# Float64 feed-forward weights written out as two ready parts, loaded straight into the last stage, and that stage's first product issued before the experts' last accumulation

## The chip, the cores and the metric

The kernel runs on one core of a Trainium2 chip. The metric is the device time of the whole program in microseconds, the median of three runs. TensorE (PE) multiplies, VectorE (DVE), ScalarE (ACT) and GpSimd (POOL) do elementwise work, and all DMA transfers are issued by SyncE (SP), whose queue takes them in order.

## The reference

Attention with a decay feeds eight experts whose outputs are summed with a gate that a few rounds of normalising produce, and their sum feeds one dense layer with a mish activation. Only the last two parts matter here.

```python
def _moe_ref(x, w_gate, w1, w2):          # x [1152, 512], w1 [8, 512, 1024], w2 [8, 1024, 512]
    ...
    for e in range(E):
        h = np.maximum(x @ w1[e], 0.0)
        ye = h @ w2[e]
        out += P[:, e:e + 1] * ye
    return out.astype(np.float32)

def _moe2_ref(x, w_in, w_out):            # w_in [512, 2048], w_out [2048, 512], both float64
    h = x @ w_in
    sp = np.where(h > 20.0, h, np.log1p(np.exp(np.minimum(h, 20.0))))
    g = h * np.tanh(sp)
    return (g @ w_out).astype(np.float32)
```

`w_in` and `w_out` become float64 through the division by a numpy square root, so the kernel receives them as 64-bit words.

## The kernel before, in words

Every product is made of three: a float32 operand is split into a high part, rounded to the multiplier's format, and a low part, the difference, and the product is high by high, high by low and low by high (`l1`, `l2`).

**Weights.** They come in halves of 512 hidden columns: halves 0 to 15 are the experts' (two each), halves 16 to 19 the dense layer's. Four slots hold four halves, half n in slot n modulo 4, each with the tiles `w1h`, `w1l`, `w2h` and `w2l`, 1 MB each. A half comes in four loads of 512 KB into the staging tile `stg` (L76). `split` then makes each part in two pieces: ScalarE copies 512 columns into the high tile (L89), and VectorE, or GpSimd where `lo_engine` says so, subtracts (L90). Such pieces wait in the list `bg` and one is taken out in each step.

**Experts.** A step is one `l1` (12 matmuls of 384 columns into `ph`), its `relu_split` (ScalarE `hh`, VectorE `hlo`), then the `l2` of the step before (9 matmuls of 512 columns into three accumulators). There are 184 steps. After the last step of an expert and a chunk of 384 tokens, `evict` adds the three accumulators to `acc` on VectorE (L799). In the last expert, `x2_trans` transposes the finished chunks 0 and 1 on TensorE (L818), and ScalarE and VectorE write them to `xh` and `xl`, the inputs of the last stage.

**Decoding.** Between steps 11 and 137, at odd steps, `decode` turns one piece of a float64 matrix (128 x 256 words) into float32 with eight VectorE instructions and writes it to DRAM (`w_in_f`, `w_out_f`, 64 pieces of 128 KB). Halves 16 to 19 are then loaded from there and split like the others: 16 and 17 during the last expert, with VectorE subtracting, and 18 and 19 in the first eight steps of the last stage, with GpSimd subtracting, two pieces per step.

**Last stage.** There are 48 steps, three chunks of 16 groups; call them u0 to u47. Each has an `l1`, ten elementwise instructions of the mish (VectorE L885, L892, L901, L905, L906, L907, L914; ScalarE L886, L893, L894 and the copy `hh` at L909, which the VectorE subtraction `hlo` at L914 follows), and an `l2`. The code issues the `l1` of a step and then the `l2` of the step three earlier. Before the first `l1` stand four `x2_trans` of chunk 2, since its accumulators are only complete then. The scratch tiles of the mish are the accumulators `acc` 0 to 5 and two tiles `scr`.

Every engine takes its instructions in the order of the code; nothing reorders them.

Of the kernel before, what the change touches and what calls it, by code (L numbers as in the profile page):

```python
# [18 lines left out]
F2 = 2048  # L19
# [19 lines left out]
def f(ap):  # L39
    return ap.bitcast(F32)  # L40


class Weights:
    """Half-expert weights: DMA to staging, split into hi + lo, ring of slots."""

    def __init__(self, nc, stage, w1, w2, w_in, w_out):
        self.nc, self.stage = nc, stage
        self.src = (w1, w2, w_in, w_out)
        self.slots = {}
        self.raw = {}  # L50

# [6 lines left out]
        return self.slots[half % 4]  # L58

    def load(self, half, part):  # L60
        w1, w2, w_in, w_out = self.src
        t = self.stage.tile([128, 2, 512], F32, tag="stg", name="stg")
        kk = part % 2
        if half < 2 * E:
            e, a = divmod(half, 2)
            if part < 2:
                src = w1[e, kk * 256:(kk + 1) * 256, a * 512:(a + 1) * 512]
            else:
                src = w2[e, a * 512 + kk * 256:a * 512 + (kk + 1) * 256, :]
        else:  # L70
            a = half - 2 * E
            if part < 2:
                src = w_in[kk * 256:(kk + 1) * 256, a * 512:(a + 1) * 512]
            else:
                src = w_out[a * 512 + kk * 256:a * 512 + (kk + 1) * 256, :]
        self.nc.sync.dma_start(out=t, in_=src.rearrange("(k p) n -> p k n", p=128))  # L76
        self.raw[half, part] = t

    def split(self, half, part, j, lo_engine=None, how=None):
        nc = self.nc  # L80
# [18 lines left out]
def attention_moe_kernel(  # L99
# [23 lines left out]

    xh = [xpool.tile([128, KD, CH], FR, name=f"xh{c}") for c in range(NCH)]
    xl = [xpool.tile([128, KD, CH], FR, name=f"xl{c}") for c in range(NCH)]
    w_in_f = dram.tile([DM, F2], F32, name="w_in_f")
    w_out_f = dram.tile([F2, DM], F32, name="w_out_f")
    wts = Weights(nc, stage, w1, w2, w_in_f, w_out_f)
    wts.add_slot(0, slot_a)

    idn = const.tile([128, 128], F32, name="idn")
# [502 lines left out]
    for i in (1, 2, 3):  # L634
        wts.add_slot(i, slot_b)
    acc += [accb.tile([128, DM], F32, name=f"acc{j}") for j in range(6, NT)]
    ps_h = mctx.enter_context(tc.tile_pool(name="ps_h", bufs=2, space=PSUM))
    ps_a = mctx.enter_context(tc.tile_pool(name="ps_a", bufs=5, space=PSUM))
    ps_m = mctx.enter_context(tc.tile_pool(name="ps_m", bufs=1, space=PSUM))

    def l1(half, ft_, c):
        w = wts.get(half)
        fs = slice(ft_ * 128, (ft_ + 1) * 128)
        ph = ps_h.tile([128, 512], F32, tag="h", name="ph")[:, :CH]
        for kk in range(KD):
# [68 lines left out]
        raw64.append((raw, dst, j))  # L714

    def decode():
        """One piece of a float64 matrix, taken as its raw words, to float32 (nearest even)."""
        raw, dst, j = raw64.pop()
        d2 = dst.rearrange("(p a) n -> p (a n)", p=128)
        a_ = dec.tile([128, 256], F32, tag="da", name="da")  # L720
        b_ = dec.tile([128, 256], F32, tag="db", name="db")
        ai, bi = a_.bitcast(U32), b_.bitcast(U32)
        lw, hw = raw[:, :, 0], raw[:, :, 1]
        v = nc.vector
        v.tensor_scalar(out=ai, in0=hw, scalar1=0x7FFFFFFF, scalar2=None, op0=ALU.bitwise_and)
        v.tensor_scalar(out=a_, in0=a_, scalar1=TINY, scalar2=HUGE, op0=ALU.max, op1=ALU.min)
        v.tensor_scalar(
            out=ai, in0=ai, scalar1=0x38000000, scalar2=4, op0=ALU.bitwise_xor, op1=ALU.logical_shift_left
        )
        v.tensor_scalar(out=bi, in0=hw, scalar1=0x80000000, scalar2=None, op0=ALU.bitwise_and)  # L730
        v.scalar_tensor_tensor(
            out=ai, in0=ai, scalar=1, in1=bi, op0=ALU.logical_shift_right, op1=ALU.bitwise_or
        )
        v.tensor_scalar(out=bi, in0=ai, scalar1=0xFF800000, scalar2=None, op0=ALU.bitwise_and)
        v.scalar_tensor_tensor(out=b_, in0=lw, scalar=2.0 ** -52, in1=b_, op0=ALU.mult, op1=ALU.mult)
        v.tensor_tensor(out=a_, in0=a_, in1=b_, op=ALU.add)
        nc.sync.dma_start(out=d2[:, j * 256:(j + 1) * 256], in_=a_)
        if decodes:
            fetch(*decodes.pop(0))

    decodes = [(w_in, w_in_f, j) for j in range(DM * F2 // (128 * 256))]
    decodes += [(w_out, w_out_f, j) for j in range(DM * F2 // (128 * 256))]
    bg = []
    dmaq = []
    side = [sinkhorn()]
# [32 lines left out]
    for half in range(2, 20):  # L778
        queue_load(half)
    queue_split(1, nc.gpsimd)  # L780
    psa = {}
# [45 lines left out]
    for idx, (e, c, g, first, last) in enumerate(steps):  # L827
        if first and (c == 0 and e > 0 or idx == 0):
            if e < E - 1:
                queue_split(2 * e + 2)  # L830
                queue_split(2 * e + 3)
            else:
                queue_split(16)
                queue_split(17)
        if c > 0 and g == 2 and e == E - 1:
            tq += [(c - 1, kk) for kk in range(KD)]
        half, gg = 2 * e + g // 4, g % 4
        ph = l1(half, gg, c)
# [19 lines left out]
    l2(*prev[0])
    evict(*prev[1])
    mctx.close()  # L860

# [1 line left out]
    fctx = ExitStack()  # L863
    ps_h = fctx.enter_context(tc.tile_pool(name="ps_h2", bufs=4, space=PSUM))
    ps_a = fctx.enter_context(tc.tile_pool(name="ps_a2", bufs=4, space=PSUM))
    for t in bg:
        t()
    bg.clear()
    queue_split(18, nc.gpsimd)
    queue_split(19, nc.gpsimd)  # L870
    scr2 = fctx.enter_context(tc.tile_pool(name="scr2", bufs=1))
    free = [a_[:, :CH] for a_ in acc[:6]] + [scr2.tile([128, CH], F32, name=f"scr{i}") for i in range(2)]
    scr = {"m": free[:1], "e": free[1:4], "w": free[4:6], "a": free[6:8]}

    def scratch(tag):
        t = scr[tag].pop(0)
        scr[tag].append(t)
        return t

    osb = acc[6:9]  # L880

    def mish_a(u):
        m = scratch("m")
        e_ = scratch("e")
        nc.vector.tensor_scalar(out=m, in0=u["ph"], scalar1=20.0, scalar2=None, op0=ALU.min)  # L885
        nc.scalar.activation(out=e_, in_=m, func=AF.Exp)  # L886
        u["e"] = e_

    def mish_w(u):
        e_ = u["e"]  # L890
# [23 lines left out]
        nc.vector.tensor_tensor(out=hl, in0=u["g"], in1=f(u["hh"]), op=ALU.subtract)  # L914
        u["hl"] = hl

    for kk in range(KD):
        x2_trans(NCH - 1, kk, ps_h, "h")
    steps = [(c, g) for c in range(NCH) for g in range(F2 // 128)]

    def finish(c):
# [9 lines left out]
    for idx in range(len(steps) + 3):  # L931
# [8 lines left out]
        if idx < len(steps):  # L940
            c, g = steps[idx]
            half, gg = 16 + g // 4, g % 4
            u = dict(half=half, gg=gg, c=c, first=g == 0, last=g == F2 // 128 - 1)
            us.append(u)
            u["ph"] = l1(half, gg, c)
        if idx < len(steps):
            mish_a(u)
        if 2 <= idx < len(steps) or idx == len(steps) + 1:
            mish_d(us[idx - 2])
        if idx < len(steps):  # L950
            for _ in range(2):
                if bg:
                    bg.pop(0)()
# [39 lines left out]
```

## Time and profile before

| | |
|---|---|
| device time, median of 3 runs | 1175.01 us (1175.01 to 1175.04) |
| span of the profiled execution | 1173.7 us |
| TensorE busy | 1138.0 us (97%) |
| VectorE busy | 732.7 us (62%) |
| ScalarE busy | 392.3 us (33%) |
| GpSimd busy | 119.0 us (10%) |
| DMA | 82.08 MB, mean 70 GB/s |

The profile is of one execution and shows its span, from the first instruction to the last; it does not show a separate time of that execution, so the 1.3 us between span and median stand for what lies around it. Busy shares are means over stages with different limits: attention lasts to about 185 us, the experts to about 953 us, the last stage to the end. A busy TensorE is not TensorE at its peak, since matmuls overlap and their ends are modelled; the distance from the start of one group of matmuls to the start of the next says more.

### The profile page before, as it was taken

To read this page: it belongs to the slowest core of one execution; us is meant where nothing else is said; L and a number is where in the kernel's file an instruction comes from. 1 tells how busy PE (TensorE), PEld (TensorE's weight loads), DVE (VectorE), ACT (ScalarE), POOL (GpSimd) and SP (SyncE) were. 2 spreads that over 40 slices of the span, in tenths; PEclk is the share of its full clock that TensorE was granted. 3 is DMA by queue.
4 is the path that set the end of the run, shared out by engine and by line. 5 is a ranking of instruction groups with operands and counts; after the bars stand their busy time and mean duration, and the time that the engine had idled before them with its cause. 6 is when DMAs were issued, how large, how long until landed. Compare 5 with 4: busy or idle time off the path is not lost.

```text
span 1173.7 us, 16305 instructions
## 1 busy us (share of the span) xinstructions
PE 1138.0 (97%) x6200; PEld 1010.1 (86%) x6200; DVE 732.7 (62%) x1707; ACT 392.3 (33%) x832; POOL 119.0 (10%) x143
## 2 busy tenths in 40 slices
PE   5899999999999999999999999999999988999998
PEld 4677788999999999999999999999999976899997
DVE  7866655776646655664665575533134259998887
ACT  6756653322212211221221221122123235555554
POOL 5734433000000000000000000000000015100000
PEclk9989999999999999999999999999999999999999
DMA  6424212333313321331332232212011012000000
GB/s 153 113 48 94 52 47 66 104 114 109 114 53 100 102 90 61 125 95 55 112 108 64 86 118 85 63 56 71 1 54 61 30 35 74 1 28 1 27 1 27
DMA packets 77759, 82.08 MB, mean 70 GB/s; under 512 B 34912, under 2 KB 46944, under 8 KB 77680
## 3 DMA queue, kind: packets, MB, share of 16 engines
q1 hardware_dynamic: 77680, 81.03, 23.1%
q8 instruction: 49, 0.80, 0.3%
q14 instruction: 30, 0.25, 0.1%
HBM read 66.00 MB, written 10.82 MB: 65 GB/s over the span
## 4 chain that ended last, share of the span: by engine, by line
PE 91%; DVE 6%; ACT 1%; issue 1%; DMA 1%; POOL 0%; SPq 0%; ACTq 0%; DVEq 0%; POOLq 0%
PE ph L647 39%; PE pa L667 39%; PE x L430 3%; PE pt L406 2%; PE sp L354 2%; PE pa L499 2%; PE ph L480 2%; PE pt L318 1%; PE sp L355 1%; DVE scr L905 1%; DVE scr L906 1%; DVE scr L907 0%; DVE acc L892 0%; DVE scr L901 0%; ACT hh L909 0%
## 5 line engine op out<-in xcount | busy, mean ns | idle before, releaser
L647 PE MATMUL ph<-xh,w1h 128*128 128x384 f32 x928 | 312.3, 337 | 0.2 <-DVE xl L822 0.2
L647 PE MATMUL ph<-xh,w1l 128*128 128x384 f32 x928 | 311.8, 336 | 0.0
L647 PE MATMUL ph<-xl,w1h 128*128 128x384 f32 x928 | 311.3, 335 | 0.0
L657 DVE SCALAR_TENSOR_TENSOR hlo<-ph,hh 128x384 fp32r<-128x384 f32 x184 | 102.8, 558 | 317.6 <-ACT hh L656 317.6
L656 ACT ACTIVATE hh<-ph 128x384 fp32r<-128x384 f32 x184 | 90.7, 493 | 588.9 <-PE ph L647 581.7
L667 PE MATMUL pa<-w2h,hh 128*128 128x512 f32 x696 | 274.1, 394 | 10.6 <-ACT hh L909 10.6
L667 PE MATMUL pa<-w2l,hh 128*128 128x512 f32 x696 | 273.4, 393 | 0.0
L667 PE MATMUL pa<-w2h,hlo 128*128 128x512 f32 x696 | 272.9, 392 | 0.0
L647 PEld LDWEIGHTS ph<-xh,w1h 128*128 128x128 f32 x928 | 174.3, 188 | 9.4 <-DVE xl L822 0.5
L647 PEld LDWEIGHTS ph<-xl,w1h 128*128 128x128 f32 x928 | 174.3, 188 | 8.5
L647 PEld LDWEIGHTS ph<-xh,w1l 128*128 128x128 f32 x928 | 174.3, 188 | 0.0
L667 PEld LDWEIGHTS pa<-w2h,hh 128*128 128x128 f32 x696 | 131.0, 188 | 33.0 <-ACT hh L909 13.4
L667 PEld LDWEIGHTS pa<-w2h,hlo 128*128 128x128 f32 x696 | 131.0, 188 | 30.4 <-DVE hlo L914 2.6
L667 PEld LDWEIGHTS pa<-w2l,hh 128*128 128x128 f32 x696 | 131.2, 188 | 19.1
L90 POOL TENSOR_TENSOR w1l<-stg,w1h 128x512 fp32r<-128x512 f32 x12 | 17.4, 1473 | 782.1 <-DVE acc L892 756.7
L390 POOL TENSOR_SCALAR p<-p,rs 128x256 f32<-128x256 f32 (+6 forms) x80 | 46.6, 594 | 66.9 <-DVE rs L386 41.5
L377 ACT ACTIVATE p<-p,nmax 128x256 f32<-128x256 f32 (+6 forms) x80 | 48.2, 604 | 9.6 <-DVE nmax L367 8.7
L799 DVE SCALAR_TENSOR_TENSOR acc<-pa,P,acc 128x512 f32<-128x512 f32 x69 | 47.5, 743 | 1.7 <-PE pa L667 1.7
L367 DVE CUSTOM_DVE_ANT_0 p<-sp,mask 128x256 f32<-128x256 f32 (+6 forms) x80 | 38.0, 476 | 12.6 <-PE sp L355 10.5
L89 ACT CAST w1h<-stg 128x512 fp32r<-128x512 f32 x76 | 45.8, 612 | 0.0
L89 ACT CAST w2h<-stg 128x512 fp32r<-128x512 f32 x76 | 45.8, 612 | 0.0
L90 DVE TENSOR_TENSOR w1l<-stg,w1h 128x512 fp32r<-128x512 f32 x64 | 44.1, 692 | 0.1
(150 smaller groups left out, 1200.0 us busy)
## 6 DMA issues: line engine op xcount, KB each, us to landing
stg<-in_moe_w_dram SPq DMA_DIRECT2D x64, 512.0 KB
raw<-in_moe_w_in_dram SPq DMA_DIRECT2D x32, 256.0 KB
raw<-in_moe_w_out_dram SPq DMA_DIRECT2D x32, 256.0 KB
w_in_f<-da SPq DMA_DIRECT2D x32, 128.0 KB
w_out_f<-da SPq DMA_DIRECT2D x32, 128.0 KB
stg<-w_in_f SPq DMA_DIRECT2D x8, 512.0 KB
stg<-w_out_f SPq DMA_DIRECT2D x8, 512.0 KB
out_dram<-acc SPq DMA_DIRECT2D x9, 256.0 KB
```

Of the source, the lines that this page charges most:

```text
L89: nc.scalar.copy(out=hi, in_=raw)
L90: (lo_engine or nc.vector).tensor_tensor(out=lo, in0=raw, in1=f(hi), op=ALU.subtract)
L354: nc.tensor.matmul(out=t[:n, :w], lhsT=a1, rhs=kt[:, h, ks], start=True, stop=False)
L367: nc.vector.tensor_tensor_reduce(out=p[:n, a, o:o + w], in0=t[:n, :w], in1=mask[:n, m0 + o:m0 + o + w], scale=-1.0, scalar=prev, op0=ALU.a ...
L377: nc.scalar.activation(out=p[:n, a, :nk], in_=p[:n, a, :nk], func=AF.Exp, bias=prev, scale=-1.0, accum_out=u["ssum"][:n, a:a + 1],)
L390: nc.gpsimd.tensor_scalar(out=p[:n, a, :nk], in0=p[:n, a, :nk], scalar1=r[:n, a:a + 1], scalar2=1.0, op0=ALU.mult, op1=ALU.mult,)
L430: nc.tensor.matmul(out=x[64 * a:64 * a + 64, h // 2, :n], lhsT=vts[b, j][:w, h + a, :], rhs=pT[:w, a, j * n:(j + 1) * n], start=j == 0, st ...
L647: nc.tensor.matmul(out=ph, lhsT=w[wn][:, kk, fs], rhs=x[c][:, kk], start=(kk == 0 and n == 0), stop=(kk == KD - 1 and n == 2),)
L656: nc.scalar.activation(out=hh, in_=ph, func=AF.Relu)
L657: nc.vector.scalar_tensor_tensor(out=hl, in0=ph, scalar=0.0, in1=f(hh), op0=ALU.max, op1=ALU.subtract)
L667: nc.tensor.matmul(out=pa[j], lhsT=a_[:, ts_], rhs=w[wn][:, ft_, :], start=(first and n == 0), stop=(last and n == 2),)
L799: nc.vector.scalar_tensor_tensor(out=acc[t], in0=pa, scalar=sc, in1=acc[t], op0=ALU.mult, op1=ALU.add)
```

## The change

`decode` no longer writes its float32 piece. At the following even step a new function `part` makes the high part on ScalarE and the low part on VectorE, 256 columns each, and writes both to DRAM; there are now four DRAM tensors, `w_in_h`, `w_in_l`, `w_out_h` and `w_out_l`. A new method `direct` loads a half of the dense layer with four DMAs of 1 MB straight into its slot, with no staging and no `split`. Halves 16 and 17 are issued at step (7, 1, 0), 15 steps before the experts' last; half 18 after the experts' last step and half 19 after its accumulation.

The first `l1` of the last stage, u0, is issued before the experts' last `l2`, with the first two of its mish instructions, and its `ph` comes from the experts' pool. The four `x2_trans` of chunk 2 move from in front of the last stage into its steps 7, 9, 11 and 13; they are needed from step 32 on.

```diff
+    def direct(self, half):
+        a = half - 2 * E
+        for n, src in (("w1", self.ready[0]), ("w2", self.ready[1])):
+            for m, s in zip("hl", src):
+                s = s[:, a * 512:(a + 1) * 512] if n == "w1" else s[a * 512:(a + 1) * 512, :]
+                self.nc.sync.dma_start(
+                    out=f(self.get(half)[n + m]), in_=s.rearrange("(k p) n -> p k n", p=128)
+                )
...
-        nc.sync.dma_start(out=d2[:, j * 256:(j + 1) * 256], in_=a_)
         if decodes:
             fetch(*decodes.pop(0))
+        decoded.append((a_, b_, dst, j))
+
+    def part():
+        a_, b_, dst, j = decoded.pop()
+        nc.scalar.copy(out=b_.bitcast(FR), in_=a_)
+        nc.vector.tensor_tensor(out=a_.bitcast(FR), in0=a_, in1=b_, op=ALU.subtract)
+        for t, d in zip((b_, a_), dst):
+            d2 = d.rearrange("(p a) n -> p (a n)", p=128)
+            nc.sync.dma_start(out=d2[:, j * 256:(j + 1) * 256], in_=t)
...
-            else:
-                queue_split(16)
-                queue_split(17)
...
+        if e == E - 1 and c == 1 and g == 0:
+            wts.direct(16)
+            wts.direct(17)
...
             decode()
+        elif decoded:
+            part()
...
-    queue_split(18, nc.gpsimd)
-    queue_split(19, nc.gpsimd)
...
+    wts.direct(18)
+    u0 = dict(half=2 * E, gg=0, c=0, first=True, last=False, ph=l1(2 * E, 0, 0))
+    mish_a(u0)
     l2(*prev[0])
     evict(*prev[1])
+    wts.direct(19)
     mctx.close()
...
-    for kk in range(KD):
-        x2_trans(NCH - 1, kk, ps_h, "h")
+    tq = [(NCH - 1, kk) for kk in range(KD)]
...
+        if 6 <= idx and idx % 2 and tq:
+            x2_trans(*tq.pop(0), ps_a, "a")
```

On TensorE, before, at the end of the experts: L667 is `l2`, L818 the transposes of chunk 2, L647 the first `l1` of the last stage.

```order
L667 MATMUL pa<-w2l_2483,hh 128x512
L667 MATMUL pa<-w2h_2482,hlo 128x512
L818 MATMUL x_8851<-idn,acc_2484 128x128
L818 MATMUL x_8851<-idn,acc_2485 128x128
...
L818 MATMUL x_8869<-idn,acc_2486 128x128
L647 MATMUL ph<-xh_75,w1h_83 128x384
L647 MATMUL ph<-xl_78,w1h_83 128x384
```

And with the change, where L671 is `l2` and L651 is `l1`; `w2h_2484` lies in slot 3, the experts' last half, and `w1h_85` in slot 0, half 16.

```order
L671 MATMUL pa<-w2h_2484,hlo 128x512
L651 MATMUL ph<-xh_75,w1h_85 128x384
L651 MATMUL ph<-xl_78,w1h_85 128x384
L651 MATMUL ph<-xh_75,w1l_86 128x384
...
L671 MATMUL pa<-w2h_2484,hh 128x512
L671 MATMUL pa<-w2l_2485,hh 128x512
```

The twelve matmuls of u0 have moved between the last two `l2` of the experts, and the transposes are gone from here.

On VectorE, before, at the same place: L799 is the experts' last accumulation, L822 the low part of the transposed chunk, L885 and L892 the first mish instructions.

```order
L799 SCALAR_TENSOR_TENSOR acc_2484<-pa,P,acc_2484 128x512
L799 SCALAR_TENSOR_TENSOR acc_2485<-pa,P,acc_2485 128x512
L799 SCALAR_TENSOR_TENSOR acc_2486<-pa,P,acc_2486 128x512
L822 TENSOR_TENSOR xl_80<-x_8851,xh_77 128x384
...
L822 TENSOR_TENSOR xl_80<-x_8869,xh_77 128x384
L885 TENSOR_SCALAR acc_98<-ph 128x384
L892 SCALAR_TENSOR_TENSOR acc_102<-acc_99 128x384
L885 TENSOR_SCALAR acc_98<-ph 128x384
L901 SCALAR_TENSOR_TENSOR scr_8849<-acc_102,acc_99 128x384
```

With the change, where L887, L909, L918 and L922 are what L885, L892, L901 and L905 were, and L813 what L799 was:

```order
L887 TENSOR_SCALAR acc_100<-ph 128x384
L813 SCALAR_TENSOR_TENSOR acc_2486<-pa,P,acc_2486 128x512
L813 SCALAR_TENSOR_TENSOR acc_2487<-pa,P,acc_2487 128x512
L813 SCALAR_TENSOR_TENSOR acc_2488<-pa,P,acc_2488 128x512
L909 SCALAR_TENSOR_TENSOR acc_104<-acc_101 128x384
L887 TENSOR_SCALAR acc_100<-ph 128x384
L918 SCALAR_TENSOR_TENSOR scr_9021<-acc_104,acc_101 128x384
L909 SCALAR_TENSOR_TENSOR acc_105<-acc_102 128x384
L922 SCALAR_TENSOR_TENSOR scr_9021<-scr_9021,acc_101 128x384
```

The first mish instruction of u0 stands ahead of the accumulation, its second behind it, and its third behind the first instruction of u1.

On SyncE, with the change, from the last decoded piece to the first loads of the dense layer (L751 is a write of `part`, L70 an expert's load, L79 a load of `direct`):

```order
L751 DMA w_out_h<-db 128x256
L751 DMA w_out_l<-da 128x256
L70 DMA stg<-in_moe_w_dram 128x2x512 x5
L79 DMA w1h_85<-w_in_h 128x4x512
L79 DMA w1l_86<-w_in_l 128x4x512
L79 DMA w2h_87<-w_out_h 128x4x512
```

Sixteen such loads follow one another there, where sixteen loads into `stg` stood, each of which waited for a staging tile.

## Rows read from the trace of the kernel before

**Rows 1.** Windows of the last stage: each engine's busy us, clock, DMA.

```profile
953.00:1006.00 53.00, 41.91 (x200) 35.19 (x201) 47.58 (x64) 27.67 (x54) 25.18 (x16) 0.97 0.19 60
1006.00:1160.00 154.00, 154.00 (x785) 140.51 (x784) 135.93 (x268) 84.01 (x157) 0.00 (x0) 1.00 0.03 11
```

**Rows 2.** Chain that ended last, in order of time: start us, us, what.

```profile
933.43 0.33 PE x L818 x3
...
948.90 2.75 PE pa L667 x12
...
951.67 2.12 DVE acc L799 x3
...
955.60 2.37 PE ph L647 x12
...
957.99 0.57 DVE acc L885
...
959.10 1.03 ACT w1h L89 x2
...
961.24 1.43 DVE scr L901
962.67 1.58 DVE acc L892
964.25 1.57 DVE scr L905
...
967.03 0.52 ACT hh L909
...
1002.83 2.48 PE pa L667 x9
1005.31 2.08 PE ph L647 x12
1007.39 2.05 PE pa L667 x9
```

**Rows 3.** TensorE in order of time: start, us, what, [idle before, releaser].

```profile
967.59 0.70 PE L667 MATMUL pa<-w2h,hh 128*128 128x512 f32 x1 [3.40 <-ACT hh L909]
...
971.34 0.33 PE L647 MATMUL ph<-xh,w1h 128*128 128x384 f32 x1
...
979.27 0.50 PE L667 MATMUL pa<-w2h,hh 128*128 128x512 f32 x1 [1.33 <-ACT hh L909]
```

**Rows 4.** Windows of two us inside that stretch, columns as in rows 1.

```profile
969.00:971.00 2.00, 2.00 (x6) 1.62 (x5) 1.97 (x3) 1.19 (x3) 2.00 (x2) 0.50 0.00 0
...
975.00:977.00 2.00, 2.00 (x12) 1.87 (x11) 1.97 (x2) 1.04 (x2) 2.00 (x2) 1.00 0.04 8
```

**Rows 5.** VectorE in order of time, an early step and a later one.

```profile
974.78 1.67 DVE L905 SCALAR_TENSOR_TENSOR scr<-scr,acc 128x384 f32<-128x384 f32 x1
976.48 1.55 DVE L906 TENSOR_TENSOR scr<-acc,scr 128x384 f32<-128x384 f32 x1
...
1058.92 0.55 DVE L905 SCALAR_TENSOR_TENSOR scr<-scr,acc 128x384 f32<-128x384 f32 x1
...
1061.19 0.56 DVE L885 TENSOR_SCALAR acc<-ph 128x384 f32<-128x384 f32 x1 [0.53 <-PE ph L647]
```

**Rows 6.** GpSimd in order of time, the same early step.

```profile
974.40 3.21 POOL L90 TENSOR_TENSOR w2l<-stg,w2h 128x512 fp32r<-128x512 f32 x2 [2.62 <-DVE scr L901]
```

**Rows 7.** Windows of one us after a 512 KB load issued at 898.76.

```profile
900.00:901.00 1.00, 1.00 (x8) 1.00 (x7) 0.46 (x1) 0.00 (x0) 0.00 (x0) 1.00 0.67 176
901.00:902.00 1.00, 1.00 (x7) 0.87 (x6) 0.00 (x1) 0.53 (x2) 0.00 (x0) 1.00 0.85 332
```

**Rows 8.** VectorE in order of time, an odd experts' step with a decode.

```profile
607.54 0.56 DVE L657 SCALAR_TENSOR_TENSOR hlo<-ph,hh 128x384 fp32r<-128x384 f32 x1 [2.94 <-ACT hh L656]
...
611.08 0.42 DVE L736 TENSOR_TENSOR da<-da,db 128x256 f32<-128x256 f32 x1
```

**Rows 9.** SyncE in order of time: the next load into staging after that decode.

```profile
617.03 0.38 SPq L76 DMA_DIRECT2D stg<-in_moe_w_dram  x1
```

More of the change, by code (lines that the diff above doesn't have):

```diff
@@ L47, in __init__ @@
         self.nc, self.stage = nc, stage
-        self.src = (w1, w2, w_in, w_out)
+        self.src = (w1, w2)
+        self.ready = (w_in, w_out)
         self.slots = {}
@@ L60, in load @@
     def load(self, half, part):
-        w1, w2, w_in, w_out = self.src
+        w1, w2 = self.src
         t = self.stage.tile([128, 2, 512], F32, tag="stg", name="stg")
         kk = part % 2
[L64 to L67, printed above, removed]
-            else:
-                src = w2[e, a * 512 + kk * 256:a * 512 + (kk + 1) * 256, :]
-        else:
[L71 to L75, printed above, removed]
+        e, a = divmod(half, 2)
+        if part < 2:
+            src = w1[e, kk * 256:(kk + 1) * 256, a * 512:(a + 1) * 512]
+        else:
+            src = w2[e, a * 512 + kk * 256:a * 512 + (kk + 1) * 256, :]
         self.nc.sync.dma_start(out=t, in_=src.rearrange("(k p) n -> p k n", p=128))
         self.raw[half, part] = t
+    def direct(self, half):
[6 more added lines that the diff above has]
+                )
     def split(self, half, part, j, lo_engine=None, how=None):
@@ L125, in attention_moe_kernel @@
     xl = [xpool.tile([128, KD, CH], FR, name=f"xl{c}") for c in range(NCH)]
-    w_in_f = dram.tile([DM, F2], F32, name="w_in_f")
-    w_out_f = dram.tile([F2, DM], F32, name="w_out_f")
-    wts = Weights(nc, stage, w1, w2, w_in_f, w_out_f)
+    w_in_s = [dram.tile([DM, F2], F32, name=f"w_in_{n}") for n in "hl"]
+    w_out_s = [dram.tile([F2, DM], F32, name=f"w_out_{n}") for n in "hl"]
+    wts = Weights(nc, stage, w1, w2, w_in_s, w_out_s)
     wts.add_slot(0, slot_a)
@@ L636, in attention_moe_kernel, with l1 @@
     acc += [accb.tile([128, DM], F32, name=f"acc{j}") for j in range(6, NT)]
-    ps_h = mctx.enter_context(tc.tile_pool(name="ps_h", bufs=2, space=PSUM))
+    ps_h = ctx.enter_context(tc.tile_pool(name="ps_h", bufs=2, space=PSUM))
     ps_a = mctx.enter_context(tc.tile_pool(name="ps_a", bufs=5, space=PSUM))
     ps_m = mctx.enter_context(tc.tile_pool(name="ps_m", bufs=1, space=PSUM))
-    def l1(half, ft_, c):
+    def l1(half, ft_, c, pool=None):
         w = wts.get(half)
         fs = slice(ft_ * 128, (ft_ + 1) * 128)
-        ph = ps_h.tile([128, 512], F32, tag="h", name="ph")[:, :CH]
+        ph = (pool or ps_h).tile([128, 512], F32, tag="h", name="ph")[:, :CH]
         for kk in range(KD):
@@ L718, in decode @@
         raw, dst, j = raw64.pop()
-        d2 = dst.rearrange("(p a) n -> p (a n)", p=128)
-        a_ = dec.tile([128, 256], F32, tag="da", name="da")
-        b_ = dec.tile([128, 256], F32, tag="db", name="db")
+        a_ = dec.tile([128, 256], F32, tag="da", name="da", bufs=2)
+        b_ = dec.tile([128, 256], F32, tag="db", name="db", bufs=2)
         ai, bi = a_.bitcast(U32), b_.bitcast(U32)
@@ L736, in decode @@
         v.tensor_tensor(out=a_, in0=a_, in1=b_, op=ALU.add)
-        nc.sync.dma_start(out=d2[:, j * 256:(j + 1) * 256], in_=a_)
         if decodes:
             fetch(*decodes.pop(0))
-    decodes = [(w_in, w_in_f, j) for j in range(DM * F2 // (128 * 256))]
-    decodes += [(w_out, w_out_f, j) for j in range(DM * F2 // (128 * 256))]
+        decoded.append((a_, b_, dst, j))
[6 more added lines that the diff above has]
+            nc.sync.dma_start(out=d2[:, j * 256:(j + 1) * 256], in_=t)
+    decoded = []
+    decodes = [(w_in, w_in_s, j) for j in range(DM * F2 // (128 * 256))]
+    decodes += [(w_out, w_out_s, j) for j in range(DM * F2 // (128 * 256))]
     bg = []
@@ L777, in attention_moe_kernel @@
     queue_load(1, skip=2)
-    for half in range(2, 20):
+    for half in range(2, 2 * E):
         queue_load(half)
@@ L831, in attention_moe_kernel @@
                 queue_split(2 * e + 3)
-            else:
-                queue_split(16)
-                queue_split(17)
         if c > 0 and g == 2 and e == E - 1:
@@ L857, in attention_moe_kernel @@
         prev = ((half, gg, psa[e, c], hh, hl, first, last), (e, c))
[L858 to L868, printed above, removed]
-    queue_split(18, nc.gpsimd)
-    queue_split(19, nc.gpsimd)
-    scr2 = fctx.enter_context(tc.tile_pool(name="scr2", bufs=1))
-    free = [a_[:, :CH] for a_ in acc[:6]] + [scr2.tile([128, CH], F32, name=f"scr{i}") for i in range(2)]
-    scr = {"m": free[:1], "e": free[1:4], "w": free[4:6], "a": free[6:8]}
+    assert not (bg or raw64 or decoded)
+    wts.direct(18)
+    free = [a_[:, :CH] for a_ in acc[:6]]
+    scr = {"m": free[:1], "e": free[1:4], "w": free[4:6]}
     def scratch(tag):
@@ L878, in scratch @@
         return t
-    osb = acc[6:9]
     def mish_a(u):
@@ L887, in mish_a @@
         u["e"] = e_
+    u0 = dict(half=2 * E, gg=0, c=0, first=True, last=False, ph=l1(2 * E, 0, 0))
+    mish_a(u0)
+    l2(*prev[0])
+    evict(*prev[1])
+    wts.direct(19)
+    mctx.close()
+    fctx = ExitStack()
+    ps_h2 = fctx.enter_context(tc.tile_pool(name="ps_h2", bufs=2, space=PSUM))
+    ps_a = fctx.enter_context(tc.tile_pool(name="ps_a2", bufs=4, space=PSUM))
+    scr2 = fctx.enter_context(tc.tile_pool(name="scr2", bufs=1))
+    scr["a"] = [scr2.tile([128, CH], F32, name=f"scr{i}") for i in range(2)]
+    osb = acc[6:9]
     def mish_w(u):
@@ L943, in attention_moe_kernel @@
             u = dict(half=half, gg=gg, c=c, first=g == 0, last=g == F2 // 128 - 1)
+            u = u if idx else u0
             us.append(u)
-            u["ph"] = l1(half, gg, c)
-        if idx < len(steps):
-            mish_a(u)
+            if idx:
+                u["ph"] = l1(half, gg, c, (ps_h, ps_h2)[idx // 2 % 2])
+                mish_a(u)
         if 2 <= idx < len(steps) or idx == len(steps) + 1:
             mish_d(us[idx - 2])
[L950 to L953, printed above, removed]
+        if 6 <= idx and idx % 2 and tq:
+            x2_trans(*tq.pop(0), ps_a, "a")
         if idx >= 3:
```

## The prediction

> **What bounds the kernel now.** I read the windows by stage first. From 1006 to 1160 us TensorE is busy in 154.00 of 154 us; from 953 to 1006 only in 41.91 of 53, with its clock at 0.97 and GpSimd busy for 25.18 us [rows 1]. So the last stage is bound by TensorE except in its first 50 us. A step there costs 2.08 us for the twelve matmuls of `l1` and 2.05 for the nine of `l2`, 4.13 together [rows 2].
>
> The chain that ended last says who holds TensorE in the first 50 us. It leaves TensorE at 951.67 for the experts' last accumulation, comes back for the transposes and the `l1` of u0 at 955.60, then runs over VectorE's mish instructions and `hh`, and returns to TensorE for good at 1002.83, with the next `l1` at 1005.31 [rows 2]. TensorE's timeline shows the waits: 3.40 us in front of the `l2` of u0 at 967.59, and 1.33 us in front of a later one at 979.27, for `hh` both times [rows 3]. From 979.27 to 1002.83 there are four steps, so a step lasts 5.89 us there instead of 4.13.
>
> Why VectorE is late there: L905 and L906 last 1.67 and 1.55 us at 974.78 and 976.48, and L905 lasts 0.55 at 1058.92 [rows 5]. Beside the long ones GpSimd makes two weight pieces, 3.21 us from 974.40 on [rows 6]. After that VectorE has room: at 1061.19 it waits 0.53 us for TensorE [rows 5].
>
> **What the lost time consists of.** From the experts' last but one `l2` at 948.90 to the `l1` of u10 at 1005.31 pass 56.41 us [rows 2]. TensorE's own work in them, without transposes, is two `l2` of the experts (4.10), ten `l1` (20.80) and seven `l2` of the stage (14.35): 39.25. The other 17.16 us are five pieces:
> - 2.60 from the end of the last `l2` (948.90 + 4.10 = 953.00) to 955.60, accumulation and transposes;
> - 3.67 in front of the `l2` of u0 (967.59 less 955.60 less four `l1`, 8.32);
> - 1.70 because this `l2` then lasts from 967.59 to 971.34, 3.75 us, at a granted clock of 0.50, so 1.2 GHz, after 3.40 us without work [rows 3, 4];
> - 8.76 in the five steps from 973.42 (971.34 + 2.08) to 1002.83, 29.41 instead of 20.65;
> - 0.43 in the last `l2`, 2.48 instead of 2.05.
>
> **The change part by part.**
>
> *u0 ahead of the last `l2`.* It needs half 16 and chunk 0, which are ready, and a `ph` that the step before last has released. The accumulation ends at 953.79 (951.67 + 2.12), 0.79 after the last `l2`; behind it now lies the `l1` of u1, 2.08 us, so TensorE no longer stands still: the 2.60 go, except for the transposes. Only the `l1` of u2 waits for the accumulators' banks, and it starts after 2.08.
>
> *Transposes.* Three matmuls cost 0.33 us [rows 2], in four steps: 1.32 come back. Their ScalarE copy and VectorE subtraction now stand in VectorE's queue in steps 7 to 13; VectorE's 0.53 of free time per step and the reserve of the three steps between `l1` and `l2` cover them.
>
> *No pieces in the last stage.* With GpSimd silent and ScalarE's two casts gone (1.03 us at 959.10), L901, L892 and L905 at 961.24 to 965.83 lose about 0.9, 1.1 and 1.0 us [rows 2], and the slow steps fall to TensorE's 4.13. This returns the 8.76 and the 0.43.
>
> *The ramp.* From the end of the `l1` of u0 to its `hh` passed 9.58 us (957.97 to 967.55); less 3.0 for the three long VectorE instructions and 1.03 for the casts, 5.5 us of chain are left. In the new order TensorE has the last `l2` and three `l1` to do before it wants this `hh`: 2.05 + 6.24 = 8.29. But VectorE's queue has more: the second instruction of u0 stands behind the accumulation (2.05 + 0.79 = 2.84 after the `l1` of u0), the third behind the first of u1, which waits for the `l1` of u1 (4.13), and between third and fourth stands the second of u1, which waits for ScalarE (about 5.4). From there three instructions and `hh`, about 2.9: some 8.4 us, 0.1 to 0.2 late. I take 0.2; the bounds are 0 and the old 3.67, with another 1.70 if the clock falls again.
>
> *`part`.* 64 subtractions of 256 columns, 0.42 us each like L736, and 64 copies, under the 0.52 of the 384-column `hh`. The odd step waits 2.94 us for `hh` when it comes to its `hlo` [rows 8]: the even step before it has this much room. I cost it at nothing; without this room it would be 64 x 0.42 = 27 us. The two writes wait on SyncE for ScalarE and VectorE. Behind them stands the next load into staging; it is issued at 617.03, while the even step's first instructions, `part` among them, come some 4 us earlier [rows 8, 9]. Nothing waits.
>
> *Loads.* 16 MB instead of 8, in DMAs of 1 MB. The windows after a load of 512 KB show 176 and 332 GB/s [rows 7]; at the lower one a half of 4 MB takes 24 us. Halves 16 and 17 are issued 15 steps, over 60 us, ahead. Half 18 can start when the experts are through with slot 2, three steps or about 13 us before 953, and is wanted by u8 at about 980 (950.95 + 2.08 + 2.05 + 6.24 + 5 x 2.05 + 4 x 2.08 + 0.33); half 19 starts behind it and is wanted by u12 at about 997. All hidden: 0.
>
> *Sum.* 17.16 - 1.32 - 0.2 = 15.6 us off the span of 1173.7, which with 1.3 around it makes the median of 1175.0: **1159.4 us**.
>
> Whether it is GpSimd that lengthens the VectorE instructions, and not the transfers that land in those steps, decides whether larger transfers are harmless. L906 lasted 1.55 us at 976.48, in a window with GpSimd busy throughout and a DMA share of 0.04 [rows 4, 5]: GpSimd it is. The Trainium skill, SBUF — State Buffer, section Who interferes with whom, says the same: a VectorE instruction with two SBUF inputs and a GpSimd instruction that reads SBUF exclude each other for a whole instruction, and a DMA never contends with an engine. By that rule the sum stands; if transfers were the cause, it would lose what the second rival gives.
>
> **Rivals.**
> 1. *The ramp still waits.* VectorE starts its mish behind an accumulation and meets the transposes' copies in steps 7 to 13, each of which it must wait for. For it: my margin is negative by 0.2 us. Against: without GpSimd each step gains 0.5 us on TensorE. At worst the old stall and the clock return, 5.4 us: up to 1164.8.
> 2. *The transfers slow VectorE.* For it: long instructions and transfers share the early steps. Against: the window named above. Halves 18 and 19 are 8 MB, 25 us at 332 and 48 at 176 GB/s: four to eight steps at 1.76 us (5.89 - 4.13) lost, 1166 to 1173.
> 3. *Slower: late weights.* One queue brings 6 MB (half 18 and the first two parts of half 19) between about 940 and 997. Below 110 GB/s u12 waits; below 86 GB/s (6.3 MB in 57 + 15.6 us) the kernel is slower than before; at 80 GB/s it gives 1181. Against: both windows of rows 7 are far above.
>
> **How the numbers follow.** Forecast 0.76, own range 1158.9 to 1160.6 (no stall at all, or one of over 1 us); first rival 0.16, between 1160.6 and 1164.8; second 0.04; third 0.04. The range goes from 1158.6 to 1163.0: it takes in the forecast and the better half of the first rival. A measurement here can tell about 0.2%, 2.35 us, from no change. Faster: 0.76 + 0.16 + half of the second rival = 0.94; same, where its price is highest, 0.02; slower 0.04.
>
> **What the profile of the changed kernel would show.** GpSimd idle after attention's end and the first weight pieces; L922 and L923 (once L905 and L906) at 0.55 us in every step; `l1` of u0 between the last two `l2`, no idle TensorE at the transition, and under 1 us in front of the `l2` of u0; clock 1.00 throughout; `l1` of u10 about 40 us after the last but one `l2` of the experts instead of 56.41; the experts' steps still 4.13 us apart, or 4.46 with a transpose. I am wrong if TensorE waits for a DMA of L79, if VectorE's instructions stay long without GpSimd, or if the experts' steps grow where `part` runs.

## The result and the profile after

The changed kernel takes 1156.2 us (median of 4 runs, 1155.9 to 1161.29) against 1175.01 (1174.63 to 1175.04): a ratio of 0.9853, with a 95% interval of 0.9833 to 0.9873. The forecast was 1159.4 with a range of 1158.6 to 1163.0. The direction was right, but the median lies 3.2 us below the forecast and 2.4 us below the range: 18.8 us were gained where the sum had 15.6.

The stretch in which the change works first. The windows of the changed kernel, with the columns of [rows 1]: us, busy us of PE, PEld, DVE, ACT, POOL, granted clock, DMA share, GB/s.

```profile
953.00:1006.00 53.00, 53.00 (x276) 48.09 (x275) 48.79 (x96) 29.53 (x58) 0.00 (x0) 1.00 0.10 39
1006.00:1140.00 134.00, 134.00 (x683) 122.31 (x682) 117.04 (x232) 72.72 (x134) 0.00 (x0) 1.00 0.03 13
```

TensorE is now busy throughout, GpSimd is silent and the clock stays at 1.00, where 11 us of the first window were empty before. The chain of the changed kernel, start us, us, what, has the place of [rows 2]:

```profile
181.78 2.10 PE ph L651 x12
...
944.80 2.05 PE pa L671 x9
946.85 2.08 PE ph L651 x12
948.93 2.05 PE pa L671 x9
950.98 6.24 PE ph L651 x36
957.23 2.35 PE pa L671 x9
...
974.07 0.33 PE x L832 x3
...
985.10 2.08 PE ph L651 x12
```

The `l1` of u0 lies at 946.85 between the last two `l2` of the experts; three `l1` follow at 950.98 without a gap, and the `l2` of u0 at 957.23 lasts 2.35 instead of 2.05, so 0.3 us are lost there. From the last but one `l2` of the experts (944.80) to the `l1` of u10 (985.10) are 40.30 us, where [rows 2] have 56.41; two more transposes, 0.66, come after that. The change is thus worth 56.41 - 40.30 - 0.66 = **15.45 us** in its own stretch, against 15.6 in the sum.

VectorE's early instructions and a later one, in the changed kernel:

```profile
953.58 0.55 DVE L918 SCALAR_TENSOR_TENSOR scr<-acc,acc 128x384 f32<-128x384 f32 x1
...
954.73 0.55 DVE L922 SCALAR_TENSOR_TENSOR scr<-scr,acc 128x384 f32<-128x384 f32 x1
955.31 0.56 DVE L923 TENSOR_TENSOR scr<-acc,scr 128x384 f32<-128x384 f32 x1
...
972.20 0.56 DVE L931 TENSOR_TENSOR hlo<-scr,hh 128x384 fp32r<-128x384 f32 x1 [0.17 <-ACT hh L926]
```

L922 and L923 are the L905 and L906 of [rows 5], 0.55 us from the first step on. The loads of halves 18 and 19 run beside them; these windows are of the changed kernel too:

```profile
935.00:940.00 5.00, 5.00 (x29) 4.59 (x29) 1.34 (x3) 0.97 (x2) 0.00 (x0) 1.00 0.94 334
...
950.00:955.00 5.00, 5.00 (x30) 4.85 (x29) 4.01 (x8) 1.91 (x5) 0.00 (x0) 1.00 0.89 286
955.00:960.00 5.00, 5.00 (x26) 4.22 (x25) 4.71 (x10) 3.08 (x6) 0.00 (x0) 1.00 0.69 268
960.00:965.00 5.00, 5.00 (x28) 4.63 (x27) 4.60 (x10) 2.99 (x6) 0.00 (x0) 1.00 0.00 0
```

Transfers of 268 to 334 GB/s end before 965, more than 10 us ahead of u8 (its `l1` starts at 976.49), and VectorE's 0.55 us at 953.58 to 955.31 fall into them.

**Where the rest is.** The first `l1` of the experts starts at 181.78 now. Before, the chain has it at 185.85:

```profile
185.85 2.10 PE ph L647 x12
```

So 4.07 us come out of attention, of which the change touches nothing: TensorE's instructions there are the same in the same order. From there to the last but one `l2` it is 763.05 us before (948.90 less 185.85) and 763.02 after. 4.07 and 15.45 make the 19.6 by which the two spans differ (1173.7 and 1154.1). Windows of attention, the kernel before:

```profile
54.00:56.00 2.00, 1.26 (x15) 1.05 (x15) 2.00 (x5) 0.82 (x2) 0.97 (x2) 1.00 0.34 75
56.00:58.00 2.00, 2.00 (x9) 1.50 (x8) 1.39 (x7) 1.86 (x5) 1.47 (x2) 0.59 0.07 18
58.00:60.00 2.00, 2.00 (x9) 1.20 (x10) 0.42 (x1) 1.27 (x4) 1.14 (x2) 0.50 0.06 14
...
66.00:68.00 2.00, 2.00 (x15) 1.60 (x16) 1.21 (x3) 1.09 (x3) 0.00 (x0) 0.85 0.00 0
```

And the changed kernel:

```profile
46.00:48.00 2.00, 1.13 (x12) 0.72 (x12) 1.97 (x8) 1.23 (x4) 1.15 (x2) 0.94 1.22 208
48.00:50.00 2.00, 2.00 (x9) 1.75 (x8) 0.76 (x4) 0.45 (x3) 1.96 (x3) 0.50 0.81 135
50.00:52.00 2.00, 2.00 (x17) 1.22 (x15) 1.10 (x2) 1.50 (x4) 0.85 (x2) 0.71 0.00 0
```

The granted clock fell to 0.50 (1.2 GHz) in both, for about 10 us in the one and 3.4 in the other. Shortly before the long fall TensorE waited 1.71 us for VectorE, until 54.74. Whether this difference belongs to the change is what the experiments have to tell first.

### The profile page after: what moved, and what is told of

Its sections match the earlier page's. It is cut to its first block, busy times and chain, and to the rows that moved or that the text cites. A ratio compares the mean times of both kernels' runs of the same rounds, so it can differ in the third digit from the quotient of the medians.

```text
span 1154.1 us, 16607 instructions
## 1 busy us (share of the span) xinstructions
PE 1131.4 (98%) x6200; PEld 1008.2 (87%) x6200; DVE 726.4 (63%) x1755; ACT 395.1 (34%) x864; POOL 94.4 (8%) x127
## 4 chain that ended last, share of the span: by engine, by line
PE 95%; DVE 3%; ACT 1%; DMA 1%; issue 0%; POOL 0%; SPq 0%; ACTq 0%; DVEq 0%; POOLq 0%
PE ph L651 42%; PE pa L671 41%; PE x L434 3%; PE pt L410 2%; PE sp L358 2%; PE pa L503 2%; PE ph L484 1%; PE pt L322 1%; PE sp L359 1%; PE x L832 0%; DVE p L371 0%; DVE xl L441 0%; DMA qb<-cd 0%; DVE rs L389 0%; PE g L450 0%
## 5 line engine op out<-in xcount | busy, mean ns | idle before, releaser
L651 PE MATMUL ph<-xh,w1h 128*128 128x384 f32 x928 | 312.5, 337 | 0.0
L651 PE MATMUL ph<-xh,w1l 128*128 128x384 f32 x928 | 312.2, 336 | 0.0
L651 PE MATMUL ph<-xl,w1h 128*128 128x384 f32 x928 | 311.7, 336 | 0.0
L671 PE MATMUL pa<-w2h,hh 128*128 128x512 f32 x696 | 273.4, 393 | 0.6 <-ACT hh L926 0.6
L671 PE MATMUL pa<-w2l,hh 128*128 128x512 f32 x696 | 272.9, 392 | 0.0
L671 PE MATMUL pa<-w2h,hlo 128*128 128x512 f32 x696 | 272.0, 391 | 0.0
L651 PEld LDWEIGHTS ph<-xh,w1h 128*128 128x128 f32 x928 | 174.5, 188 | 8.9
L651 PEld LDWEIGHTS ph<-xl,w1h 128*128 128x128 f32 x928 | 174.5, 188 | 8.5
L651 PEld LDWEIGHTS ph<-xh,w1l 128*128 128x128 f32 x928 | 174.5, 188 | 0.0
L671 PEld LDWEIGHTS pa<-w2h,hlo 128*128 128x128 f32 x696 | 130.7, 188 | 28.7 <-DVE hlo L931 0.9
L671 PEld LDWEIGHTS pa<-w2h,hh 128*128 128x128 f32 x696 | 130.9, 188 | 21.2 <-ACT hh L926 1.6
L671 PEld LDWEIGHTS pa<-w2l,hh 128*128 128x128 f32 x696 | 130.9, 188 | 18.8
L813 DVE SCALAR_TENSOR_TENSOR acc<-pa,P,acc 128x512 f32<-128x512 f32 x69 | 47.5, 744 | 0.1
L910 ACT ACTIVATE acc<-acc,two 128x384 f32<-128x384 f32 x48 | 29.6, 617 | 48.6 <-DVE acc L909 48.6
L358 PE MATMUL sp<-kt,qa 128*128 128x256 f32 (+6 forms) x96 | 38.5, 405 | 1.7 <-DVE kt L287 1.7
L434 PEld LDWEIGHTS x<-pT,v 128*64 128x64 f32 (+1 forms) x480 | 25.1, 140 | 16.1 <-ACT pT L283 6.3
L434 PE MATMUL x<-pT,v 128*64 128x128 f32 (+3 forms) x480 | 36.4, 280 | 2.6 <-ACT pT L283 1.3
```

Source lines behind the costliest of these rows:

```text
L358: nc.tensor.matmul(out=t[:n, :w], lhsT=a1, rhs=kt[:, h, ks], start=True, stop=False)
L434: nc.tensor.matmul(out=x[64 * a:64 * a + 64, h // 2, :n], lhsT=vts[b, j][:w, h + a, :], rhs=pT[:w, a, j * n:(j + 1) * n], start=j == 0, st ...
L651: nc.tensor.matmul(out=ph, lhsT=w[wn][:, kk, fs], rhs=x[c][:, kk], start=(kk == 0 and n == 0), stop=(kk == KD - 1 and n == 2),)
L671: nc.tensor.matmul(out=pa[j], lhsT=a_[:, ts_], rhs=w[wn][:, ft_, :], start=(first and n == 0), stop=(last and n == 2),)
L813: nc.vector.scalar_tensor_tensor(out=acc[t], in0=pa, scalar=sc, in1=acc[t], op0=ALU.mult, op1=ALU.add)
L910: nc.scalar.activation(out=e_, in_=w_, func=AF.Ln, bias=two)
```

## The experiments

**Theory A**: the 15.45 us are the change; the clock in attention falls for a long or a short time from execution to execution, whatever the kernel, and the two kernels were compared at different falls. **Theory B**: the change itself shortens attention. Within the change: GpSimd's subtractions slowed VectorE (my theory), against the transfers, ScalarE's casts, or the order at the transition as the larger part.

**The changed kernel again** (`after_rep`, no edit). 

> The changed kernel again, nothing edited. Theory A: the part of the gain that my sum lacks lies in attention, where the same instructions ran at a granted clock of 0.50 for some 10.4 us in the profile of before and 3.4 us in that of after; where and how long the clock falls there differs from execution to execution, so among the runs both 1156 and 1161 us appear, the second with a clock of 0.994 like the profile of before. Theory B: the change itself makes attention faster, so all runs give 1156 and the profile always shows the short fall.

Measured: 1156.04, 1159.41, 1159.92, 1155.92 and 1156.16 us. Its profile, at 1156.04, shows no fall at all:

```profile
44.00:48.00 4.00, 2.53 (x22) 1.64 (x21) 3.87 (x12) 3.12 (x8) 2.49 (x4) 1.00 1.04 268
48.00:52.00 4.00, 4.00 (x31) 3.23 (x32) 3.43 (x8) 2.87 (x9) 3.72 (x5) 1.00 0.22 46
52.00:56.00 4.00, 2.28 (x20) 1.45 (x19) 3.96 (x9) 1.68 (x5) 2.38 (x3) 1.00 0.30 68
56.00:60.00 4.00, 4.00 (x32) 3.02 (x32) 2.49 (x9) 3.71 (x10) 2.61 (x3) 1.00 0.14 33
```

One kernel shows both levels, as A says: a lower one near 1156 us and an upper one near 1160. No fall costs as much as the short one (spans 1154.2 and 1154.1). TensorE's wait near 54 us shows why; the rows are of the kernel before, the changed kernel and `after_rep`:

```profile
54.74 0.87 PE L430 MATMUL x<-pT,v 128*64 128x128 f32 x10 [1.71 <-DVE pT L283]
54.54 0.87 PE L434 MATMUL x<-pT,v 128*64 128x128 f32 x10 [0.27 <-DVE pT L287]
54.58 0.87 PE L434 MATMUL x<-pT,v 128*64 128x128 f32 x10 [1.72 <-DVE pT L287]
```

After the short fall the wait is 0.27 us instead of 1.72, so what the clock lost there was waiting time anyway. The rows show something else too: the wait of 1.7 us stands ahead of the long fall in the kernel before, and ahead of no fall in `after_rep`.

The kernel before, run beside it, has both levels too: of its 13 runs between 1171 and 1176 us six lie at 1171.3 to 1172.7 and seven at 1174.75 to 1175.44; two more took 1178.0 and 1270.0. The mean granted clock of a whole run goes with its level. In these runs of the kernel before it is 0.997 to 0.999 at the lower level and 0.993 or 0.994 at the upper one; in the nine runs of the changed kernel so far it is 0.998 to 1.000 and 0.994 to 0.996. The changed kernel was not profiled at its upper level, so that its long fall lies in attention too is inferred. The 1175.01 of the comparison is the upper level, the 1156.2 the lower one.

**No stop of TensorE in attention** (`before_warm`, `after_warm`): in each kernel matmuls that nobody reads, ahead of the last six attention products of the second and third query tile (two in the second, four in the third).

```diff
             x = u["tile"]["x"]
+            if u["ti"] == 2 or u["ti"] == 1 and h >= 4:
+                dm = ps_f.tile([128, 512], F32, tag="fb", name="dm")
+                for _ in range(2):
+                    nc.tensor.matmul(out=dm[:, :256], lhsT=idn, rhs=mask[:, :256], start=True, stop=True)
```

> The kernel before, with two extra matmuls whose result nobody reads ahead of each of the last six attention products of the second and third query tile, so that TensorE does not stand still there. Theory A: the clock does not fall in attention, which gives back about 5 us and costs 0 to 2 us of extra matmuls: 1170 to 1172. Theory B (the clock is not what differs): 1175 to 1177.

> The changed kernel with the same extra matmuls. Theory A: it gives back only the short fall, 1.7 us, less 0 to 2 us: 1154.5 to 1156.5, and stands 15.5 us (15 to 16) below the kernel before with the same matmuls, which is the sum of my terms. Theory B: it stands 18.8 us below it.

Measured: 1172.92 us (1172.45 to 1173.15, ten runs) and 1157.47 (1157.29 to 1157.54, four runs), 15.45 us apart. They lie 0.9 us above the expected 1172 and 1.0 above the expected 1156.5: the extra matmuls cost more than I gave them. The experts now start at 183.44 and 183.12 us in the two profiles, so attention lasts nearly the same in both. The gap agrees with the 15.45 us read from the chain (to the hundredth by chance, since the lighter pair below gives 15.24); B's 18.8 is excluded. The windows of `before_warm` where the long fall was:

```profile
56.00:58.00 2.00, 2.00 (x17) 1.48 (x14) 1.95 (x7) 1.23 (x3) 0.80 (x1) 1.00 0.00 0
58.00:60.00 2.00, 2.00 (x13) 1.48 (x14) 1.23 (x5) 1.81 (x6) 1.81 (x3) 1.00 0.14 33
```

**Ready parts alone** (`parts_only`): the changed kernel with u0 and the transposes where they were.

```diff
-    u0 = dict(half=2 * E, gg=0, c=0, first=True, last=False, ph=l1(2 * E, 0, 0))
-    mish_a(u0)
...
-    tq = [(NCH - 1, kk) for kk in range(KD)]
+    for kk in range(KD):
+        x2_trans(NCH - 1, kk, ps_a, "a")
...
-            if idx:
-                u["ph"] = l1(half, gg, c, (ps_h, ps_h2)[idx // 2 % 2])
-                mish_a(u)
+            u["ph"] = l1(half, gg, c, (ps_h, ps_h2)[idx // 2 % 2])
+            mish_a(u)
```

> The changed kernel with the first product of the last stage and the four transposes put back to where they were, so only the ready-made parts are left of the change. By my sum the transition costs 2.6 us again and the transposes in the steps 1.3 less, so with the short fall in attention 1157.5 (1157 to 1158.5), with the long one 5 us more. A rival, that u0 ahead of the accumulation is worth more than that because the ramp waits without it: 1160 or more with the short fall.

Measured: 1157.31 and, three times, 1160.84 to 1161.04, the two levels again. At the lower one it is 1.2 us above the changed kernel's 1156.1, as the terms 2.60 - 1.32 say. That is a single run, but its chain agrees: from the experts' last but one `l2` (945.09) to the `l1` of u10 (987.18) it has 42.09 us, 14.32 less than the 56.41 of [rows 2], with all four transposes inside both. So the ready parts carry some 14 of the 15.45 us. The upper level lies 3.6 us above the lower one, where I expected 5.

**The order alone** (`order_warm`): the kernel before with the extra matmuls, u0 ahead and the transposes in the steps, and the pieces of halves 18 and 19 still split with GpSimd.

```diff
+    u0 = dict(half=2 * E, gg=0, c=0, first=True, last=False, ph=l1(2 * E, 0, 0))
+    mish_a(u0)
     l2(*prev[0])
     evict(*prev[1])
...
     queue_split(18, nc.gpsimd)
     queue_split(19, nc.gpsimd)
...
+        if 6 <= idx and idx % 2 and tq:
+            x2_trans(*tq.pop(0), ps_a, "a")
```

> The kernel before with the extra matmuls in attention (1172.9 without the change), and of the change only the order: first product of the last stage ahead of the experts' last accumulation, transposes in steps 7 to 13; the pieces of halves 18 and 19 are still split in the last stage, with GpSimd subtracting. My theory: the five slow steps stay, since GpSimd holds VectorE there, and only part of the transition comes back: 1169 to 1171.6. Rival, that the order is most of the gain: below 1165.

Measured: 1170.9 us (1169.31 to 1171.05, ten runs), 2.0 below `before_warm`. TensorE's waits, of `order_warm` (L671 is `l2`), start, us, what, [idle before, releaser]:

```profile
965.78 0.50 PE L671 MATMUL pa<-w2h,hh 128*128 128x512 f32 x1 [1.34 <-ACT hh L915]
971.67 0.50 PE L671 MATMUL pa<-w2h,hh 128*128 128x512 f32 x1 [1.32 <-ACT hh L915]
977.56 0.50 PE L671 MATMUL pa<-w2h,hh 128*128 128x512 f32 x1 [1.33 <-ACT hh L915]
```

Steps of 5.89 us, as in [rows 3]: without the ready parts the new order starts the slow steps earlier and leaves them as they are. Behind the last of them the clock falls once more: the `l2` at 996.06 waits 1.84 us and then lasts 3.95 instead of 2.05. Two of the ten runs, at 1169.3 with a mean clock of 1.000, may lack that fall; neither was profiled. The rival is out, at 1169.3 as at 1170.9.

**GpSimd alone back** (`pool_warm`): `after_warm`, and in eight steps of the last stage three GpSimd subtractions whose result nobody uses.

```diff
+    ds = stage.tile([128, 2, 512], F32, tag="stg", name="ds")
+    nc.gpsimd.memset(ds, 0.0)
...
+        if 2 <= idx < 10:
+            for _ in range(3):
+                nc.gpsimd.tensor_tensor(out=ds[:, 0, :CH], in0=ds[:, 1, :CH], in1=f(us[idx - 2]["hh"]), op=ALU.subtract)
```

> The changed kernel with the extra matmuls in attention (1157.5), and three GpSimd subtractions of 384 columns in each of the steps 2 to 9 of the last stage, whose result nobody uses; no casts on ScalarE and no staging loads come back. My theory: VectorE's instructions with two SBUF inputs last 1.5 us or more beside them and the steps grow to nearly 6 us: 1164 to 1168.5. Rival, that the casts or the transfers were what slowed the steps: 1157 to 1159.

Measured: 1173.61 us (1173.43 to 1173.77, ten runs), 16.1 above `after_warm` and 5 us above the expected range. That range was too low for the "nearly 6 us" beside it, since eight steps longer by 1.8 us already make 1172; and three instructions per step hold VectorE three times, where the kernel before has two long ones. GpSimd, VectorE and TensorE of one step of `pool_warm` (its lines lie four below those of the changed kernel: L922, L913, L926 and L927 are L918, L909, L922 and L923 there):

```profile
965.02 3.90 POOL L975 TENSOR_TENSOR ds<-ds,hh 128x384 f32<-128x384 f32 x3 [2.34 <-ACT hh L930]
...
965.39 1.37 DVE L922 SCALAR_TENSOR_TENSOR scr<-acc,acc 128x384 f32<-128x384 f32 x1
966.68 1.37 DVE L913 SCALAR_TENSOR_TENSOR acc<-acc 128x384 f32<-128x384 f32 x1
967.97 1.37 DVE L926 SCALAR_TENSOR_TENSOR scr<-scr,acc 128x384 f32<-128x384 f32 x1
969.37 0.56 DVE L927 TENSOR_TENSOR scr<-acc,scr 128x384 f32<-128x384 f32 x1
...
971.19 0.50 PE L675 MATMUL pa<-w2h,hh 128*128 128x512 f32 x1 [1.70 <-ACT hh L930]
```

Exactly three VectorE instructions last 1.37 us, one for each of GpSimd's three of 1.30, and the fourth is back at 0.56. From the `l2` at 964.93 to that at 971.19 a step takes 6.26 us; 2.13 above 4.13, in eight steps, is 17.0, near the 16.1. No cast and no transfer is in it: from 960 to 1010 the windows of `pool_warm` show 0 to 3 GB/s. GpSimd's instructions are enough.

That the casts are not what slowed VectorE in the kernel before was not tested by a run, but its trace shows it. Rows of one slow step there, ScalarE, VectorE and GpSimd:

```profile
979.55 1.13 ACT L89 CAST w1h<-stg 128x512 fp32r<-128x512 f32 x2
979.73 0.55 DVE L901 SCALAR_TENSOR_TENSOR scr<-acc,acc 128x384 f32<-128x384 f32 x1
980.23 3.28 POOL L90 TENSOR_TENSOR w1l<-stg,w1h 128x512 fp32r<-128x512 f32 x2 [2.62 <-ACT w1h L89]
980.66 1.67 DVE L905 SCALAR_TENSOR_TENSOR scr<-scr,acc 128x384 f32<-128x384 f32 x1
```

L901 runs beside the casts, in a window with 238 GB/s, and lasts 0.55 us; only what follows the start of GpSimd is long. L905 and L906 together last 2.1 us more there than later [rows 5], enough for the 1.76 us by which a step grew.

**A light filler** (`after_light`, `before_light`): one extra matmul instead of two, in the third query tile only.

```diff
-            if u["ti"] == 2 or u["ti"] == 1 and h >= 4:
+            if u["ti"] == 2:
...
-                for _ in range(2):
+                for _ in range(1):
```

> The changed kernel with one extra matmul instead of two, ahead of the four attention products of the third query tile only. My theory: enough to keep the clock up where it fell for long, and cheaper than in the version with two: 1155.8 to 1157 in every run, with none at 1159 or above, where the changed kernel itself has some. Rival: too little to matter, some runs at 1159 to 1161.

> The kernel before with one extra matmul ahead of the four attention products of the third query tile, as in the light version of the changed kernel, which gave 1156.5. If the change is worth what its own stretch shows (15.5 us), 1172.0 (1171.6 to 1172.4) in nearly every run, and none at 1174.7 or above, where the kernel before itself has most of its runs. If the gain of the changed kernel came from attention too, 1175.

Measured: 1156.51 us (1156.49 to 1156.55, four runs) and 1171.75 (1171.62 to 1171.89, twelve runs), 15.24 apart. Neither has a run at its kernel's upper level. Beside `before_light`, the kernel before had ten runs at 1171.3 to 1171.7, six at 1174.75 to 1175.4 and one at 1176.84.

**A filler at one place** (`after_one`): two extra matmuls ahead of the one product at the 1.7 us wait (`u["ti"] == 2 and h == 4`). 

> The changed kernel with two extra matmuls ahead of a single attention product, the one in front of which TensorE waited 1.7 us just before the long fall of the clock in the profile of before. If that wait is what brings on the long fall: 1156.0 to 1156.5 in every run. If the shorter wait of 0.9 us some 7 us earlier also can: some runs at 1158 to 1161.

Measured: 1156.13 to 1156.23 in three runs and 1157.41 in one, which is the profiled one and fits neither expectation. There the clock fell for a short time and early, with a mean of 0.77 from 40 to 42 us, 0.50 to 44 and 0.88 to 46, and nothing fell afterwards. Ahead of it lies a wait of 0.84 us for GpSimd, until 40.66; both waits that the expectation names come later, and so do the fillers, at 53.76. The kernel before and the changed kernel have the same wait of 0.84 us there, with the clock at 1.00 behind it. Four runs without a long fall fit the view that the 1.7 us wait is needed for it, but four are too few to show it, and `after_rep` has that wait without any fall.

The changed kernel has 1159.4 to 1161.3 in three of its nine runs and 1155.9 to 1156.24 in the others; `after_light` costs 0.35 us over the lower level and has stayed off the upper one. Its mean of 1156.5 against 1157.5 makes it the better of the two, by little, and on the strength of four runs.

## Why the prediction was half right

- **The sum was right.** 15.6 us forecast, 15.45 in the chain, 15.45 and 15.24 between the two pairs of kernels with extra matmuls. Its pieces hold: the transition (`parts_only`, 1.2 us net), the transposes 0.33 each, the slow steps gone, the clock at 1.00 after u0, 0.3 us lost at the `l2` of u0 where I had 0.2.
- **The step that failed is the last line of the sum**, "off the span of 1173.7, which with 1.3 around it makes the median of 1175.0". It took the attention of that one execution as part of the kernel. That execution held a fall of the clock of some 10 us, and with it attention lasted 4.07 us longer than in the changed kernel's profile; the rows by stage that I showed begin at 953, and the range had no term for anything ahead of it. From the lower level of the kernel before, 1171.3 to 1171.7, the sum gives 1155.7 to 1156.1, which is what six of nine runs show. From the upper level, 1175.0, it gives 1159.4, near its other runs, 1159.4 to 1161.3. Had most runs of the changed kernel lain at its upper level, 1159.4 would have looked right by luck, with the same step missing.
- **"Clock 1.00 throughout"** was claimed for the changed kernel and holds from the experts on only.
- **The three runs of before agreed within 0.03 us**, and I read that as a sign of one level. They were three runs at the same one. The "0.2%, 2.35 us" that I took as what a measurement can tell is less than the 3.7 us between the levels.
- **GpSimd against transfers**: decided rightly, and now shown by adding GpSimd alone. The Trainium skill, SBUF — State Buffer, section Who interferes with whom, says that the loser blocks for a whole instruction and that a DMA never contends with an engine; the 1.37 us beside GpSimd's 1.30 agree, and so do the 0.55 us beside transfers of 268 to 286 GB/s.
- **`part` at nothing**: right. Rows of the changed kernel beside [rows 8]: the subtraction lies at 600.42 in an even step, and the next odd step still waits 2.67 us. The experts' 763.05 us before and 763.02 after say the same for the whole stretch.

```profile
600.42 0.42 DVE L748 TENSOR_TENSOR da<-da,db 128x256 fp32r<-128x256 f32 x1
603.50 0.56 DVE L661 SCALAR_TENSOR_TENSOR hlo<-ph,hh 128x384 fp32r<-128x384 f32 x1 [2.67 <-ACT hh L660]
```

- **The rivals**: the ramp hardly waits; transfers do not slow VectorE; no weight is late, as TensorE waits for no DMA of L79 in the profile of the changed kernel.

What stays open is what decides, from one execution to the next, whether the clock falls for long in attention. The instructions and their order are the same, and the fillers remove the fall without telling what sets it off. Whether the change alters how often the upper level comes is not shown either: three of the nine runs of the changed kernel have it, three of the four of `parts_only`, and of the kernel before between six runs of 17 and twelve of 19, from one set of runs to the next. The wait of 1.7 us itself comes from VectorE, here in the kernel before:

```profile
47.95 0.16 DVE L385 TENSOR_SCALAR rs<-ssum 128x2 f32<-128x2 f32 x1
50.93 2.49 DVE L385 TENSOR_SCALAR rs<-ssum 128x2 f32<-128x2 f32 x1
```

The same small instruction lasts 0.16 us once and 2.49 the next time, when two GpSimd subtractions run beside it from 50.79 to 53.39. It looks like the clash of the last stage again, in an instruction with one input; no run took it away.

## What to carry to other kernels

A sum made against one profiled execution carries that execution's accidents: before using a span as the base, look at the granted clock in every stretch, also in those that the change does not touch, and if it falls anywhere, give the time with and without the fall as two cases. GpSimd as a helper for VectorE is not free: a VectorE instruction with two SBUF inputs lasted about as long as the GpSimd subtraction beside it (1.37 us instead of 0.55), so 0.8 us of VectorE went for each 1.30 of GpSimd. Here it was better to do the work once, in an earlier stage with room, and to store the parts ready, even at twice the bytes. A few matmuls without use in front of a wait can make the time of a kernel steady, and two kernels comparable.

## What the runs showed of the hardware

- Most runs of the kernel before lie at two levels some 3.7 us apart, near 1171.5 and 1175.2 us, with the same instructions; a few lie between them or above, at 1172.6 to 1172.7 and 1176.8 to 1178.2. A fall of the granted clock to 0.50 for 3.4 us cost nothing measurable (`after`), one of about 10 us some 4 us. One run with another short fall was 1.2 us longer than the three others of its kernel (`after_one`).
- A VectorE instruction of 384 columns with two inputs from SBUF, 0.55 us alone, lasted 1.37 us beside a GpSimd subtraction of 384 columns (`pool_warm`) and 1.43 to 1.67 beside those of 512 (the kernel before), also when both inputs were the same tile. GpSimd paid too: two of its pieces of 512 columns took 3.21 us there and 2.57 at 189.26, with no such instruction beside them.
- One or two extra matmuls of 256 columns at four to six places narrowed the spread of the kernel before from over 5 us (1171.3 to 1176.8 beside the first, 1171.3 to 1178.0 beside the second, without the run of 1270.0) to 0.3 (`before_light`, twelve runs) and 0.7 us (`before_warm`, ten runs).
- Loads of 1 MB in rows of 2 KB reached 334 GB/s over five us with TensorE busy throughout, and at 268 to 286 GB/s VectorE's instructions kept their 0.55 us.
